# A new hand-written order of all steps in a windowed-attention and gated-MLP kernel on one core

## The chip, the core and the metric

The kernel runs on one core of a Trainium2 chip, in one launch. The core has five engines that run side by side, each through its own instruction queue in order: PE (TensorE, matmuls), DVE (VectorE), ACT (ScalarE), POOL (GpSimd) and SP (SyncE, which only issues DMAs here). DMAs are issued from SP's queue or from POOL's; 16 DMA engines carry them out. The metric is the device time of a whole run in microseconds (us), lower is better. Runs of this kernel on one chip differ by some tenths of a per cent.

## What is computed

Attention over 4 batches, 8 heads, 768 positions and 64 columns a head, with a window of 128 positions and 4 sink positions that every row sees; then a block with a spatial gate on its output x (4 x 768 x 512). Inputs and output are float32; the kernel computes in bfloat16 with float32 sums.

```python
scores = scale * np.matmul(q, k.transpose(0, 1, 3, 2))
is_sink = pos[None, :] < int(n_sink)
in_window = (rel >= 0) & (rel < int(window))
scores = np.where(is_sink | in_window, scores, -1000000000.0)
a = np.exp(scores - np.max(scores, axis=-1, keepdims=True))
a = a / (np.sum(a, axis=-1, keepdims=True) + 1e-09)
x = np.matmul(a, v)                      # heads side by side: B, S, 512
...
h = gelu_tanh(x @ w_in)                  # 512 -> 1024
u, v = h[..., :512], h[..., 512:]
v_n = (v - mean) / np.sqrt(var + 1e-06) * g_ln
v_s = np.einsum('ts,bsd->btd', w_sg, v_n) + b_sg[None, :, None]
out = x + (u * v_s) @ w_out
```

## The kernel before

The whole program is a list of 669 steps, `STEPS`, written out by hand. Each step is a name with indices (batch first) and at times the letter of an engine (A for ACT, D for DVE, P for POOL); a loop at L676 calls the function of that name for each in turn. An engine executes its own steps in the order of the list; semaphores hold it where a step needs another engine's result or a buffer that is still in use. So the list fixes two things: the order within each engine's queue, and which of the interchangeable engines does a copy, a mask or a product. It fixes no times.

The steps of one batch b, in the order of the data:

- Loads. For batch 0, q and k come in four pairs of heads through SP (LPQ, LPK, L245; 384 KB each, float32) and are cast to bfloat16 (CPQ, CPK, L199 to L204). For the other batches POOL issues tile loads LQ, LK (L225). v comes in two halves of four heads each (LVH, L271, POOL's queue); LC (L289, SP) loads the four sink rows of v, LG (L292) the gains. Weights: LW.0 and LW.1 the two halves of w_in (L277), LWS two halves of w_sg (L282), LWO w_out (L285), LB the bias b_sg (L301), all on POOL's queue.
- Turning q and k: TQ, TK on PE (L376 for batch 0, L382 for others), then a copy EQ, EK to SBUF; for batch 3 the DMA does it, DQ and DK on SP (L440).
- Scores: QK (L483; with a last index 1 a bias matmul at L478 puts the mask in, otherwise MK masks later), EX the exponentials on ACT (L488), MK the mask on DVE (L495) or on POOL (L498, L501). Sinks: KS, VSM on DVE, SK (L462), SX (L467). Index p of QK, EX, MK is the pair of heads, g the group of positions.
- AV sums the window and the sinks (L524, L528, L531), NR divides by the sum on DVE (L540, L541) and writes x. Batch 0 does this in three parts of two tiles of 128 positions, the others in two parts of three.
- x is turned: XT and XE in batch 0 (L550), XD by DMA on SP (L557) in the others, one for each half.
- MV (L566) multiplies by w_in's half for v and GV applies the gelu on ACT (L570); BN, RS (POOL, L588), NM and Z normalise v (Z on ACT L597 or DVE L600). MU (L607) and GU (L612) do the same for u. MV and MU come in groups g of two tiles.
- WT and WE turn w_sg once (L619). SP multiplies by it (L627; index hf is the half of the positions, dc the quarter of the columns), GT applies gain and bias on DVE (L632), GM multiplies by u on DVE or POOL (L637).
- OU (L644) multiplies by w_out, RA adds x on DVE (L648), ST stores (L667), SH stores in halves (L664). The very last tile goes in halves: OH (L657), RH (L661).
- Fillers: HM.n puts n warm matmuls (L190) ahead of the next step that takes a PSUM buffer. TBL (L309) lets ACT load the table of exp (E) or gelu (G) early; the compiler adds a load by itself wherever the next function needs another table. WARM, FILL, IDEN, MASK, MASK0, VSK, VSO and ZERO write constants at the start.

PSUM is used as two rings: two large buffers `sc` for QK, MV and MU in turn (freed by ACT's EX, GV, GU), and four small ones `mm` for all other matmul steps (freed mostly by DVE). A step takes the next buffer of its ring whatever the key, so the list also sets who waits for whose buffer. Output tiles pass through a ring of six buffers, `ot`, each free again when its store has landed. The batches overlap: while batch b is in its gate, batch b+1 is in its scores.

Of the kernel before, what the change touches and what calls it, by code (L numbers as in the profile page):

```python
# [17 lines left out]


STEPS = """  # L20
WARM LPQ.0 FILL LPK.0 LPK.1 LPQ.1 LPQ.2 LG MASK LPK.2 LPK.3 CPQ.0.A VSK LPQ.3 IDEN CPK.0.A IDEN2 MASK0 HM.9 TQ.0.0
# [694 lines left out]
```

## Time and profile before

| | us |
|---|---|
| median of 3 runs | 155.82 (155.35 to 155.89) |
| the profiled execution, whole | 155.89 |
| its span, first to last instruction | 154.2 |
| PE busy in it | 145.7 |
| DVE, ACT, POOL busy | 122.9, 100.0, 99.7 |

A profile comes from one execution; what lies between its whole time and its span is start and end of the launch. The granted clock of PE was 1.00 throughout. In the profile a row names source line, engine, operation and tiles; `PEld` is PE's weight load, which runs beside its matmuls. The page cuts the span into 40 slices and gives each engine's busy share in tenths. The chain of waits is followed back from the last instruction: at each step to what released it. Times inside an execution are counted from the span's start.

PE's first matmul starts at 1.25 us, the first AV at 16.56, the first MV at 23.45, the first SP at 38.91, the first OU at 54.20, the first step of batch 3's gate (SP.3.1.0) at 137.35; PE's last matmul ends at 150.5, and the last store is issued by 151.8.

### The profile page before, as it was taken

How to read it: one execution, taken by the hardware profiler on the slowest of the kernel's cores; microseconds unless marked ns; L12 is line 12 of the kernel's file. 1: busy time of each engine (PE TensorE's matmuls, PEld its weight loads, DVE VectorE, ACT ScalarE, POOL GpSimd, SP SyncE). 2: the span in 40 equal slices, each digit the busy share in tenths (PEclk: the TensorE clock that was granted, in tenths of full speed). 3: DMA queues.
4: the chain of work that ended last, by engine and by line, in shares of the span. 5: the costliest groups of instructions: out<-in, count | busy, mean ns of one | idle time of the engine just before them, and what ended most of it. 6: DMA issues, size and time to landing. Idle time of an engine off the chain costs nothing.

```text
span 154.2 us, 3867 instructions
## 1 busy us (share of the span) xinstructions
PE 145.7 (95%) x1540; PEld 94.5 (61%) x1554; DVE 122.9 (80%) x296; ACT 100.0 (65%) x117; POOL 99.7 (65%) x127
## 2 busy tenths in 40 slices
PE   6899899999999988999899999999999999999990
PEld 2355586879675765758466764486567644775550
DVE  4666889739989977797799887899789957867992
ACT  3699998799899766456987865369957122491000
POOL 4099799298999699999469769640798610400400
PEclk9999999999999999999999999999999999999999
DMA  4999999999999999999999399996510582410055
GB/s 158 305 351 157 154 195 204 166 189 211 148 141 154 185 155 140 147 150 156 156 223 250 81 276 177 185 190 81 211 72 1 105 221 73 150 54 20 0 203 206
DMA packets 87178, 24.67 MB, mean 160 GB/s; under 512 B 78772, under 2 KB 84920, under 8 KB 87160
## 3 DMA queue, kind: packets, MB, share of 16 engines
q0 software_dynamic: 64608, 11.01, 95.7%
q1 hardware_dynamic: 22552, 13.41, 33.0%
q8 instruction: 12, 0.20, 0.5%
q14 instruction: 6, 0.05, 0.1%
HBM read 24.81 MB, written 6.29 MB: 202 GB/s over the span
## 4 chain that ended last, share of the span: by engine, by line
PE 54%; POOL 18%; DMA 15%; ACT 4%; DVE 4%; issue 2%; SPq 1%; DVEq 0%; ACTq 0%; POOLq 0%
PE mm L627 15%; DMA v_sb<-in_v_dram 11%; PE mm L644 10%; PE sc L566 9%; PE sc L607 8%; POOL q L225 5%; POOL k L225 4%; DMA uT<-in_k_dram 4%; PE sc L483 4%; PE mm L524 3%; POOL v_sb L271 3%; PE mm L528 2%; POOL wsg_gated L637 2%; POOL P L498 2%; POOL P L501 2%
## 5 line engine op out<-in xcount | busy, mean ns | idle before, releaser
L488 ACT ACTIVATE P<-sc 128x1024 bf16<-128x1024 f32 (+1 forms) x48 | 43.4, 952 | 10.3 <-PE sc L483 10.1
L627 PE MATMUL mm<-wsgT,z 128*128 128x384 bf16 x192 | 34.4, 327 | 0.3 <-ACT z L597 0.3
L627 PEld LDWEIGHTS <-z 128*128 128x128 bf16 x192 | 17.6, 98 | 12.5 <-issue 0.7
L570 ACT ACTIVATE vt<-sc 128x1024 f32<-128x1024 f32 x12 | 12.3, 1027 | 18.4 <-PE sc L566 18.4
L632 DVE SCALAR_TENSOR_TENSOR gtmp<-mm,g_sb,b_bc 128x384 bf16<-128x384 f32 x32 | 19.0, 610 | 4.2 <-PE mm L627 4.0
L637 POOL TENSOR_TENSOR wsg_gated<-gtmp,uT 128x384 bf16<-128x384 bf16 x15 | 14.9, 1006 | 11.3 <-DVE gtmp L632 11.2
L607 PE MATMUL sc<-xT,w_in_sb 128*128 128x256 bf16 x192 | 22.1, 273 | 0.0
L566 PE MATMUL sc<-w_in_sb,xT 128*128 128x512 bf16 x92 | 21.8, 379 | 0.2
L644 PE MATMUL mm<-w_out_sb,wsg_gated 128*128 128x512 bf16 x85 | 21.2, 379 | 0.5
L498 POOL TENSOR_SCALAR_AFFINE_SELECT P<-P 128x512 bf16<-128x512 bf16 x21 | 13.7, 653 | 11.4 <-ACT P L488 11.4
L607 PEld LDWEIGHTS <-w_in_sb 128*128 128x128 bf16 x192 | 18.7, 98 | 2.9
L579 DVE BATCH_NORM_STATS2 st<-vt 128x6 f32<-128x512 f32 x24 | 15.4, 685 | 6.1 <-ACT vt L570 6.0
L541 DVE TENSOR_TENSOR x_sb<-mm,rcp 128x384 bf16<-128x384 f32 (+1 forms) x36 | 18.5, 513 | 1.2
L588 POOL TENSOR_TENSOR rs<-rs,neg_half 128x4 f32<-128x4 f32 (+1 forms) x8 | 7.1, 882 | 15.8 <-DVE rs L583 14.4
L225 POOL DMA_DIRECT2D k<-in_k_dram x18 | 16.4, 924 | 1.3 <-DMA v_sb<-in_v_dram 1.3
L648 DVE TENSOR_TENSOR ot<-mm,x_sb 128x512 f32<-128x512 f32 x23 | 15.4, 683 | 2.2 <-PE mm L644 2.2
L225 POOL DMA_DIRECT2D q<-in_q_dram x18 | 16.8, 956 | 0.0
L524 PE MATMUL mm<-v_sb,P 128*128 128x65 bf16 x192 | 16.1, 194 | 0.6 <-DVE x_sb L541 0.4
L524 PEld LDWEIGHTS <-P 128*128 128x128 bf16 x192 | 14.5, 97 | 2.5 <-DMA v_sb<-in_v_dram 0.6
L528 PE MATMUL mm<-v_sb,P 128*128 128x65 bf16 x160 | 15.4, 193 | 0.4 <-POOL P L501 0.4
L612 ACT ACTIVATE uT<-sc 128x1024 bf16<-128x1024 f32 x12 | 12.2, 1024 | 5.1 <-PE sc L607 5.1
L566 PEld LDWEIGHTS <-xT 128*128 128x128 bf16 x96 | 9.2, 98 | 10.1
(92 smaller groups left out, 242.9 us busy)
## 6 DMA issues: line engine op xcount, KB each, us to landing
out_dram<-ot SPq DMA_DIRECT2D x17, 256.0 KB, 2.5
v_sb<-in_v_dram POOLq DMA_DIRECT2D x8, 384.0 KB, 8.0
q<-in_q_dram POOLq DMA_DIRECT2D x18, 128.0 KB, 6.5
k<-in_k_dram POOLq DMA_DIRECT2D x18, 128.0 KB, 7.3
out_dram<-ot SPq DMA_DIRECT2D x14, 128.0 KB, 1.8
wsg_gated<-in_moe_w_sg_dram POOLq DMA_DIRECT2D x2, 576.0 KB, 8.4
w_in_sb<-in_moe_w_in_dram POOLq DMA_DIRECT2D x2, 512.0 KB, 9.0
uT<-in_q_dram SPq DMA_DIRECT2D x2, 384.0 KB, 3.0
```

The source lines that it names most:

```text
L225: return nc.gpsimd.dma_start(out=dst.rearrange("p (h d) -> p h d", h=H), in_=heads(src, b, i))
L488: nc.scalar.activation(out=P.new((b, p, g))[:, :, 0:w], in_=sc_ring[b, p, g][:, :, 0:w], func=AF.Exp, scale=scale)
L498: nc.gpsimd.affine_select(out=p4[:, :, :, 0:128], in_=p4[:, :, :, 0:128], compare_op=ALU.is_ge, fill=0.0, base=0, pattern=[[0, 2], [0, 2], ...
L524: nc.tensor.matmul(av[:, il, hl, :], pt[:, hl, c:c + 128], vb[:, h, i, :], start=first, stop=False)
L528: nc.tensor.matmul(av[:, il, hl, :], pt[:, hl, c:c + 128], vb[:, h, i - 1, :], start=False, stop=(i < 2 and il == n - 1 and hl == 1))
L541: nc.vector.tensor_mul(x_sb.get(b)[:, i0:i0 + n, 128 * p:128 * (p + 1)].rearrange("p t (h d) -> p t h d", h=2), av[:, :, :, 0:Dh], rcp[:, ...
L566: nc.tensor.matmul(hp[:, jl, :], xT[b][:, 2 * g + jl, c, :], w_in_sb[:, c, d_half:2 * d_half], start=(c == 0), stop=(c == KD - 1))
L607: nc.tensor.matmul(hp[:, dc // 2, 256 * (dc % 2):256 * (dc % 2 + 1)], w_in_sb[:, c, 128 * dc:128 * (dc + 1)], xT[b][:, 2 * g:2 * g + 2, c, :],
L627: nc.tensor.matmul(ps[:, 0:NH], z[b][:, si, 128 * dc:128 * (dc + 1)], wsgT[:, si, NH * hf:NH * (hf + 1)], start=(si == 0), stop=(si == NT ...
L632: nc.vector.scalar_tensor_tensor(out=gtmp.new((b, hf, dc)), in0=mm_ring["g", b, hf, dc][:, 0:NH], scalar=g_sb[:, dc:dc + 1], in1=b_bc[:, N ...
L637: (nc.vector if e == "D" else nc.gpsimd).tensor_mul(gated(b, hf)[:, dc, :], gtmp[b, hf, dc], uT[b][:, dc, NH * hf:NH * (hf + 1)])
L644: nc.tensor.matmul(ps, gated(b, hf)[:, dc, 128 * tl:128 * (tl + 1)], w_out_sb[:, dc, :], start=(dc == 0), stop=(dc == KU - 1))
```

## The change

All steps stand in a new order. The same work is done; no size, tile or buffer changes. With the order go these reassignments: batch 0's casts of q and k go from three on ACT, two on POOL and three on DVE to none, three and five; copies EK go from eight on ACT and two on DVE to three and seven, EQ from two and eight to five and five; GM from 17 on DVE and 15 on POOL to 20 and 12; WE, XE and Z change by one each; some MK change between DVE and POOL at equal numbers. Warm matmuls go from 21 to 19. TBL gets a second index, a number that only keeps the names apart, and stands at seven places, most of which no longer lie where the table changes; the compiler's own loads take their place. OH asks the ring whether the tile's buffer is taken, so that its halves can come in either order.

In the new list SP issues the pairs in the order q0, k0, LG, k1, q1, k2, q2, k3, q3 and LC behind them; LW.0 and LW.1 follow each other on POOL's queue with no load between.

The list's diff, cut; the lines left out are of the same kind:

```diff
--- before.py
+++ after.py
@@ STEPS @@
-WARM LPQ.0 FILL LPK.0 LPK.1 LPQ.1 LPQ.2 LG MASK LPK.2 LPK.3 CPQ.0.A VSK LPQ.3 IDEN CPK.0.A IDEN2 MASK0 HM.9 TQ.0.0
-TK.0.0 EQ.0.0.D EK.0.0.A VSO HM.4 QK.0.0.0 ZERO CPK.1.P QK.0.0.1.1 EX.0.0.0 LVH.0.0 EX.0.0.1 QK.0.0.2.1 CPQ.1.D TK.0.1
-EX.0.0.2 LC CPQ.2.D LVH.0.1 TQ.0.1 MK.0.0.0.D EK.0.1.A HM.1 TQ.0.2 EQ.0.1.D EQ.0.2.A HM.3 QK.0.1.0 CPK.2.A CPK.3.P
-QK.0.1.1.1 EX.0.1.0 LQ.1.0 CPQ.3.D TK.0.2 EX.0.1.1 TK.0.3 EK.0.2.D LQ.1.1 TQ.0.3 EK.0.3.A GTR EQ.0.3.D LW.0 HM.1
-QK.0.2.0 QK.0.2.1 EX.0.2.0 LK.1.0 KS.0 VSM.0 HM.3 SK.0.2 EX.0.2.1 SK.0.1 MK.0.2.0.D AV.0.0.0 LW.1 QK.0.3.0.1
-MK.0.1.0.D SX.0.1 SX.0.2 QK.0.3.1 MK.0.2.1.P GCP.D NR.0.0.0 EX.0.3.0 AV.0.0.1 AV.0.1.0 AV.0.1.1 NR.0.0.1 EX.0.3.1
-QK.0.1.2 NR.0.1.0 AV.0.2.0 AV.0.3.0 EX.0.1.2 MK.0.3.1.P NR.0.1.1 QK.0.2.2 AV.0.2.1 NR.0.2.0 EX.0.2.2 TQ.1.0 NR.0.3.0
-MK.0.1.2.P QK.0.3.2 AV.0.3.1 EQ.1.0.A NR.0.2.1 XT.0.0 NR.0.3.1 LWS.0 AV.0.0.2 EX.0.3.2 TBL.G AV.0.1.2 XE.0.0.D LK.1.1
-XT.0.1 MK.0.2.2.D MV.0.0 XE.0.1.A LK.1.2 NR.0.0.2 MK.0.3.2.D LK.1.3 NR.0.1.2 AV.0.2.2 AV.0.3.2 LQ.1.2 NR.0.2.2 GV.0.0
-MV.0.1 NR.0.3.2 LQ.1.3 BN.0.0 LWS.1 XT.0.2 GV.0.1 MU.0.1 XE.0.2.A BN.0.1 WT.0 GU.0.1 TK.1.0 MV.0.2 RS.0.1 EK.1.0.A
-LK.1.4 NM.0.1 WE.0.A WT.1 GV.0.2 LK.1.5 TK.1.1 MU.0.2 LB.P EK.1.1.A BN.0.2 Z.0.0.A LK.2.0 WT.2 GU.0.2 MU.0.0 WE.1.D
-RS.0.2 WE.2.D Z.0.1.A LQ.2.0 NM.0.2 Z.0.2.A Z.0.3.D Z.0.4.D WT.3 LQ.2.1 WT.4 GU.0.0 TBL.E WE.3.D WT.5 LQ.1.4 Z.0.5.D
-TQ.1.1 QK.1.0.0 EQ.1.1.D QK.1.1.0 LQ.1.5 SP.0.0.0 WE.4.D LK.2.1 EX.1.0.0 VSM.1 SP.0.0.1 WE.5.D EX.1.1.0 LVH.1.0
-GT.0.0.0 TK.1.2 KS.1 GT.0.0.1 QK.1.2.0 QK.1.3.0 EX.1.2.0 SP.0.0.2 LVH.1.1 GM.0.0.0.D EX.1.3.0 MK.1.2.0.D TQ.2.0
-EK.1.2.A LQ.2.2 QK.1.0.1 EQ.2.0.D QK.1.1.1 TQ.1.2 EX.1.0.1 GT.0.0.2 LWO SP.0.0.3 EQ.1.2.D EX.1.1.1 LK.2.2 MK.1.0.1.D
...
-EX.1.2.2 SP.0.1.3 NR.1.0.0 MK.1.1.2.P EX.1.3.2 NR.1.1.0 AV.1.2.0 AV.1.3.0 MK.1.0.2.P GT.0.1.3 QK.2.0.0 QK.2.1.0
-NR.1.2.0 EX.2.0.0 OU.0.0 MK.1.2.2.P NR.1.3.0 TK.2.1 RA.0.0 AV.1.0.1 XD.1.0 EK.2.1.A MK.1.3.2.P AV.1.1.1 NR.1.0.1
-AV.1.2.1 EX.2.1.0 GM.0.1.2.P NR.1.1.1 AV.1.3.1 NR.1.2.1 QK.2.2.0 LK.3.0 QK.2.3.0 EX.2.2.0 OU.0.1 NR.1.3.1 GM.0.1.3.P
-EX.2.3.0 TBL.G OU.0.2 XD.1.1 RA.0.1 GM.0.1.1.P TK.2.2 MK.2.3.0.D TQ.2.1 LVH.2.0 TQ.2.2 EQ.2.1.D MV.1.0 EQ.2.2.D LQ.3.0
-EK.2.2.D LQ.3.1 VSM.2 MU.1.0 GV.1.0 MK.2.1.0.D LVH.2.1 BN.1.0 MV.1.1 GU.1.0 LQ.3.2 RA.0.2 LQ.3.3 MK.2.0.0.D MV.1.2
-GV.1.1 MK.2.2.0.D LK.3.1 KS.2 LK.3.2 BN.1.1 MU.1.1 GV.1.2 LK.3.3 BN.1.2 RS.1.1 MU.1.2 GU.1.1 LQ.3.4 NM.1.1 Z.1.0.A
-RS.1.2 OU.0.3 GU.1.2 TBL.E LQ.3.5 NM.1.2 Z.1.1.D SK.2.0 Z.1.4.D QK.2.0.1 Z.1.2.D Z.1.3.A QK.2.1.1 Z.1.5.D OU.0.4
-RA.0.3 DK.3.0 SP.1.0.0 RA.0.4 SX.2.0 EX.2.0.1 SP.1.0.1 GT.1.0.0 DQ.3.0 EX.2.1.1 GM.1.0.0.D SP.1.1.0 MK.2.0.1.P
...
-EX.2.3.2 NR.2.3.0 QK.3.0.0 MK.2.3.2.P QK.3.1.0 GT.1.1.3 XD.2.0 EX.3.0.0 AV.2.0.1 MK.2.2.2.D AV.2.1.1 EX.3.1.0 NR.2.0.1
-AV.2.2.1 GM.1.1.3.P ST.0.1 NR.2.1.1 AV.2.3.1 ST.0.2 ST.0.5 GM.1.1.0.P SK.3.0 NR.2.2.1 QK.3.2.0 QK.3.3.0 NR.2.3.1
-EX.3.2.0 GM.1.1.2.P SP.1.0.2 EX.3.3.0 XD.2.1 SP.1.0.3 GT.1.0.2 SX.3.0 TBL.G MK.3.3.0.D MV.2.0 GM.1.0.2.P DK.3.1
-GM.1.1.1.D LK.3.4 MK.3.0.0.D OU.1.3 LVH.3.0 GV.2.0 OU.1.4 RA.1.3 LVH.3.1 OU.1.5 ST.1.3 RA.1.4 GT.1.0.3 MV.2.1 ST.1.4
-MK.3.1.0.D LK.3.5 BN.2.0 GM.1.0.3.P MV.2.2 GV.2.1 BN.2.1 MU.2.1 GV.2.2 BN.2.2 RS.2.1 MU.2.0 GU.2.1 NM.2.1 RA.1.5
-RS.2.2 MU.2.2 GU.2.0 NM.2.2 Z.2.4.D Z.2.5.D Z.2.0.A Z.2.1.D OU.1.0 GU.2.2 TBL.E Z.2.2.D MK.3.2.0.D OU.1.1 RA.1.0
...
-NR.3.2.0 NR.3.3.0 EX.3.3.2 TBL.G SP.2.0.3 MK.3.2.2.P GT.2.0.2 XD.3.0 AV.3.0.1 GT.2.0.3 MK.3.3.2.P AV.3.1.1 NR.3.0.1
-AV.3.2.1 GM.2.0.3.P NR.3.1.1 AV.3.3.1 SP.2.1.3 GM.2.0.2.D GM.2.1.1.P NR.3.2.1 OU.2.0 NR.3.3.1 GT.2.1.3 XD.3.1 OU.2.1
-RA.2.0 GM.2.1.3.P OU.2.2 GM.2.1.2.D SH.2.0.0 SH.2.0.1 RA.2.1 MV.3.0 RA.2.2 SH.2.1.0 SH.2.1.1 OU.2.3 GV.3.0 OU.2.4
-BN.3.0 MV.3.1 RA.2.3 RA.2.4 MV.3.2 SH.2.3.0 SH.2.3.1 GV.3.1 SH.2.2.0 SH.2.2.1 SH.2.4.0 SH.2.4.1 BN.3.1 OU.2.5 GV.3.2
...
-SH.2.5.0 SH.2.5.1 SP.3.1.0 GU.3.0 SP.3.1.1 GU.3.1 GT.3.1.0 SP.3.1.2 GM.3.1.0.D GT.3.1.1 SP.3.1.3 GM.3.1.1.D GT.3.1.2
-SP.3.0.0 GM.3.1.2.D SP.3.0.1 GT.3.0.0 GT.3.1.3 SP.3.0.2 GT.3.0.1 GM.3.1.3.P SP.3.0.3 GM.3.0.0.D GM.3.0.1.P GT.3.0.2
-OU.3.3 GM.3.0.2.D GT.3.0.3 OU.3.4 GM.3.0.3.D RA.3.3 OU.3.0 RA.3.4 ST.3.3 OU.3.1 RA.3.0 ST.3.4 OU.3.2 ST.3.0 RA.3.1
-OH.3.5.0 OH.3.5.1 ST.3.1 RA.3.2 ST.3.2 RH.3.5.0 SH.3.5.0 RH.3.5.1 SH.3.5.1
+WARM FILL IDEN LPQ.0 MASK MASK0 IDEN2 LPK.0 VSK CPQ.0.P CPK.0.D LG HM.9 TQ.0.0 EQ.0.0.D ZERO TK.0.0 LPK.1 VSO LPQ.1
+LVH.0.0 EK.0.0.A HM.3 QK.0.0.0 CPK.1.D CPQ.1.D LPK.2 EX.0.0.0 LPQ.2 HM.1 QK.0.0.1.1 LPK.3 EX.0.0.1 CPK.2.D TK.0.1
+LVH.0.1 QK.0.0.2.1 EK.0.1.A LK.1.1 CPK.3.P TQ.0.1 LQ.1.1 LPQ.3 LC CPQ.3.P EQ.0.1.A TK.0.2 CPQ.2.D TQ.0.2 QK.0.1.0
+EX.0.0.2 EK.0.2.D EX.0.1.0 TK.0.3 LQ.1.0 EQ.0.2.D EK.0.3.D QK.0.1.1.1 TQ.0.3 MK.0.0.0.D EX.0.1.1 LW.0 GTR KS.0
+EQ.0.3.A GCP.D QK.0.2.0 MK.0.1.0.D LW.1 QK.0.2.1 VSM.0 HM.1 AV.0.1.0 EX.0.2.0 HM.1 AV.0.0.0 SK.0.1 SK.0.2 EX.0.2.1
+HM.1 QK.0.3.0.1 SX.0.1 SX.0.2 NR.0.1.0 QK.0.3.1 MK.0.2.0.D AV.0.1.1 NR.0.0.0 AV.0.2.0 NR.0.1.1 AV.0.0.1 EX.0.3.0
+EX.0.3.1 HM.1 AV.0.3.0 MK.0.2.1.P QK.0.3.2 EX.0.3.2 NR.0.0.1 NR.0.2.0 QK.0.1.2 AV.0.0.2 AV.0.2.1 EX.0.1.2 NR.0.3.0
+XT.0.0 MK.0.3.1.P AV.0.3.1 MK.0.3.2.P NR.0.0.2 LB.P LK.1.0 NR.0.2.1 LQ.1.2 QK.0.2.2 XE.0.0.A NR.0.3.1 MK.0.1.2.D
+TQ.1.0 AV.0.3.2 XT.0.1 AV.0.1.2 NR.0.3.2 LWS.0 LQ.1.3 EX.0.2.2 EQ.1.0.A MV.0.0 LQ.2.0 MK.0.2.2.D LWS.1 XE.0.1.D
+NR.0.1.2 LK.1.2 AV.0.2.2 NR.0.2.2 GV.0.0 LK.1.3 MV.0.1 XT.0.2 MU.0.1 BN.0.0 GV.0.1 LQ.1.4 GU.0.1 XE.0.2.D BN.0.1
+MV.0.2 LQ.2.1 TK.1.0 GV.0.2 EK.1.0.D RS.0.1 MU.0.2 NM.0.1 BN.0.2 WT.1 WT.0 TBL.G.1 MU.0.0 Z.0.3.A LK.2.4 Z.0.1.A
+RS.0.2 NM.0.2 LK.2.0 WE.1.D Z.0.4.D LK.2.1 WE.0.A LQ.1.5 Z.0.2.D WT.2 WE.2.D Z.0.5.D Z.0.0.A HM.1 TQ.1.1 GU.0.2
+QK.1.0.0 WT.4 HM.1 SP.0.0.1 GU.0.0 EQ.1.1.D LK.1.4 TK.1.1 WT.3 WE.4.A LK.1.5 VSM.1 EK.1.1.D EX.1.0.0 GT.0.0.1 SP.0.0.0
+MK.1.0.0.D QK.1.1.0 QK.1.3.0 WE.3.D GT.0.0.0 GM.0.0.1.D WT.5 EX.1.1.0 TQ.2.0 QK.1.2.0 SP.0.0.2 EX.1.3.0 EX.1.2.0
+EQ.2.0.A QK.1.0.1 QK.1.3.1 MK.1.3.0.D KS.1 EX.1.0.1 WE.5.D GT.0.0.2 SP.0.0.3 LVH.1.0 GT.0.0.3 EX.1.3.1 LVH.1.1
...
+MK.1.2.1.P QK.1.2.2 AV.1.2.0 QK.1.3.2 NR.1.1.0 EX.1.2.2 SP.0.1.3 LK.2.3 MK.1.0.2.P MK.1.1.2.P NR.1.3.0 MK.1.2.2.D
+OU.0.0 NR.1.2.0 QK.2.0.0 EX.1.3.2 GT.0.1.3 QK.2.1.0 AV.1.2.1 RA.0.0 AV.1.0.1 NR.1.2.1 MK.1.3.2.P EX.2.1.0 EX.2.0.0
+NR.1.0.1 LK.2.2 XD.1.0 OU.0.1 AV.1.1.1 KS.2 LQ.2.2 QK.2.3.0 EX.2.3.0 QK.2.2.0 AV.1.3.1 GM.0.1.3.P TQ.2.2 EX.2.2.0
+RA.0.1 NR.1.1.1 GM.0.1.0.P OU.0.2 LVH.2.1 ST.0.0 MV.1.0 NR.1.3.1 VSM.3 LQ.2.3 GV.1.0 LVH.2.0 GM.0.1.1.D TK.2.1 MU.1.0
+MK.2.2.0.D VSM.2 XD.1.1 GU.1.0 LK.3.3 EQ.2.2.D MV.1.1 EK.2.1.D GM.0.1.2.D LK.3.0 MV.1.2 LQ.3.4 GV.1.1 RA.0.2 LQ.3.0
+MU.1.1 GV.1.2 MK.2.3.0.D BN.1.0 TQ.2.1 BN.1.1 BN.1.2 LK.3.5 MU.1.2 RS.1.1 NM.1.1 EQ.2.1.D RS.1.2 OU.0.3 NM.1.2 LQ.3.2
+MK.2.1.0.D LQ.3.5 GU.1.1 TK.2.2 Z.1.2.A Z.1.4.D Z.1.1.A LK.3.1 RA.0.3 OU.0.4 SK.2.0 LK.3.2 GU.1.2 QK.2.0.1 EK.2.2.D
+Z.1.0.A Z.1.3.D LQ.3.3 Z.1.5.D QK.2.1.1 MK.2.0.0.D EX.2.0.1 DK.3.0 SP.1.0.0 RA.0.4 EX.2.1.1 GT.1.0.0 SP.1.0.1 SP.1.1.0
...
+NR.2.1.0 MK.2.2.1.P QK.2.3.2 RA.0.5 EX.2.1.2 KS.3 EX.2.3.2 ST.0.3 AV.2.3.0 MK.2.0.2.P GT.1.1.2 MK.2.2.2.D NR.2.3.0
+MK.2.1.2.P AV.2.2.0 SP.1.1.3 DQ.3.2 AV.2.0.1 NR.2.2.0 QK.3.1.0 EX.3.1.0 QK.3.3.0 MK.2.3.2.P GM.1.1.1.P AV.2.1.1
+GT.1.1.3 AV.2.2.1 NR.2.0.1 EX.3.3.0 SP.1.0.3 AV.2.3.1 NR.2.1.1 QK.3.0.0 QK.3.2.0 NR.2.2.1 NR.2.3.1 GM.1.1.0.P GT.1.0.3
+EX.3.0.0 DQ.3.1 SK.3.0 SX.3.0 XD.2.0 GM.1.1.2.D GM.1.1.3.D SP.1.0.2 TBL.E.1 XD.2.1 EX.3.2.0 OU.1.3 MV.2.0 MK.3.1.0.D
+GV.2.0 MV.2.1 GV.2.1 GT.1.0.2 MV.2.2 DK.3.1 GM.1.0.2.P BN.2.0 BN.2.1 ST.0.2 MU.2.1 GV.2.2 LK.3.4 MK.3.3.0.D BN.2.2
+GU.2.1 MU.2.2 ST.0.5 ST.0.1 MU.2.0 RS.2.1 NM.2.1 RA.1.3 RS.2.2 Z.2.3.D GM.1.0.3.D LVH.3.0 NM.2.2 Z.2.1.A OU.1.5
+Z.2.0.D Z.2.5.D OU.1.1 GU.2.2 OU.1.0 GU.2.0 Z.2.4.A RA.1.5 QK.3.0.1 QK.3.2.1 MK.3.2.0.D Z.2.2.D MK.3.0.0.D RA.1.1
+OU.1.4 EX.3.0.1 SP.2.0.0 EX.3.2.1 LVH.3.1 RA.1.4 DK.3.2 MK.3.0.1.P ST.0.4 RA.1.0 GT.2.0.0 QK.3.0.2 GM.2.0.0.D QK.3.1.1
...
+NR.3.2.0 EX.3.3.2 GT.2.1.2 SP.2.0.1 GM.2.1.1.P AV.3.3.0 SP.2.0.2 NR.3.1.0 GM.2.1.0.P GT.2.0.1 SP.2.0.3 AV.3.0.1
+NR.3.3.0 AV.3.1.1 GT.2.0.2 GM.2.1.2.D EX.3.2.2 MK.3.3.2.P GT.2.0.3 NR.3.0.1 TBL.G.2 AV.3.3.1 MK.3.2.2.P NR.3.1.1
+ST.1.3 GM.2.0.3.D GM.2.0.2.P XD.3.0 TBL.E.2 AV.3.2.1 ST.1.5 SP.2.1.3 GM.2.0.1.D NR.3.3.1 OU.2.1 NR.3.2.1 TBL.G.3
+OU.2.2 GT.2.1.3 MV.3.0 GM.2.1.3.D GV.3.0 OU.2.4 RA.2.2 OU.2.3 RA.2.1 ST.1.4 OU.2.5 XD.3.1 RA.2.4 RA.2.5 BN.3.0 MV.3.1
+GV.3.1 MV.3.2 BN.3.1 GV.3.2 SH.2.2.0 RS.3.1 BN.3.2 MU.3.2 MU.3.0 SH.2.1.1 SH.2.2.1 GU.3.2 NM.3.1 Z.3.0.D Z.3.2.D
...
+RA.2.0 SH.2.5.1 TBL.E.3 SP.3.1.1 GT.3.1.2 GT.3.1.1 SH.2.0.0 SH.2.3.1 SH.2.0.1 GT.3.1.0 SH.2.4.1 SP.3.1.3 GM.3.1.1.D
+GM.3.1.2.P GT.3.1.3 GM.3.1.3.D GM.3.1.0.P SP.3.0.1 SP.3.0.3 GT.3.0.1 SP.3.0.0 SP.3.0.2 GT.3.0.3 SH.2.5.0 GM.3.0.1.D
+OU.3.3 GT.3.0.0 OU.3.4 GT.3.0.2 GM.3.0.0.D SH.2.3.0 GM.3.0.2.D GM.3.0.3.P RA.3.3 SH.2.1.0 OU.3.0 RA.3.4 RA.3.0 OU.3.1
+ST.3.3 OU.3.2 ST.3.4 ST.3.0 RA.3.1 OH.3.5.1 RA.3.2 OH.3.5.0 ST.3.1 RH.3.5.0 ST.3.2 SH.3.5.0 RH.3.5.1 SH.3.5.1 TBL.G.4
...
-    def TBL(func):
+    def TBL(func, turn):
         nc.scalar.activation(out=touch, in_=neg_half[:, 0:1], func=AF.Exp if func == "E" else AF.Gelu_apprx_tanh)
...
     def OH(b, t, h):
         hf, tl = t // 3, t % 3
-        ps = mm_ring["o", b, t] if h else fresh(mm_ring, ("o", b, t))
+        ps = mm_ring["o", b, t] if ("o", b, t) in mm_ring.held else fresh(mm_ring, ("o", b, t))
```

## The prediction

> **What bounds the kernel now.** First the page: busy shares, slices, the chain by engine.
>
> ```profile
> span 154.2 us, 3867 instructions
> PE 145.7 (95%) x1540; PEld 94.5 (61%) x1554; DVE 122.9 (80%) x296; ACT 100.0 (65%) x117; POOL 99.7 (65%) x127
> PE   6899899999999988999899999999999999999990
> PE 54%; POOL 18%; DMA 15%; ACT 4%; DVE 4%; issue 2%; SPq 1%; DVEq 0%; ACTq 0%; POOLq 0%
> ```
>
> PE is busy nearly throughout; only the first eighth, the slices around 55 us and the last two show holes. Next the chain of waits in order of time (start, us, what), its beginning and its end:
>
> ```profile
> 1.81 5.80 DMA uT<-in_k_dram
> 7.69 0.79 POOL k L204
> 8.48 8.04 DMA v_sb<-in_v_dram
> 16.56 0.25 PE mm L524 x3
> ...
> 126.23 1.73 PE mm L644 x8
> 127.96 3.45 PE sc L566 x16
> 131.41 0.86 PE mm L644 x4
> 132.28 5.24 PE sc L607 x48
> 137.52 7.80 PE mm L627 x48
> ```
>
> Until 16.6 us the chain is data: k's second pair, its cast on POOL, then V's first half, for which AV waits. From 76 us it is PE alone. The x-counts price PE's steps: MV 1.73, MU 5.24/3 = 1.75, SP 7.80/8 = 0.975, OU 0.86. From the timeline, first matmul to the next step's first: a QK 0.18 to 0.32, an AV 0.18, 0.36 or 0.54 (6, 10 or 15 matmuls), a turn of one group 0.34 to 0.54, one warm matmul 0.22. What a step takes beyond the least of its kind I call a gap. All steps at their least are 131.9 us, warm and bias matmuls 6.4, gaps 11.0: 5 of these before 19.5 us, 3.2 in nine places of at least 0.2 after 30 us, the rest some 0.09 at each change of operand shape. So behind the start a new order can win 3.2 us at most. The waits list names three such places (total, times, longest):
>
> ```profile
> PEld L524 <- DMA v_sb<-in_v_dram: 0.6, 1, 0.6
> PEld L644 <- DMA w_out_sb<-in_moe_w_out_dram: 0.4, 1, 0.4
> PE mm L528 <- POOL P L501: 0.4, 1, 0.4
> ```
>
> Last, DMA by window (length, then busy PE, PEld, DVE, ACT, POOL; clock, DMA share, GB/s), and one window of idle ACT:
>
> ```profile
> 9.00:11.00 2.00, 1.79 (x41) 1.29 (x43) 1.51 (x3) 2.00 (x3) 2.00 (x2) 1.00 1.04 383
> 11.00:12.00 1.00, 1.00 (x13) 0.37 (x8) 0.99 (x2) 0.98 (x3) 0.90 (x2) 1.00 1.29 173
> 97.00:99.50 2.50, 2.50 (x13) 1.16 (x12) 1.95 (x6) 1.02 (x1) 1.74 (x2) 1.00 1.87 192
> 102.00:104.00 2.00, 2.00 (x21) 1.79 (x20) 1.78 (x8) 1.28 (x2) 0.89 (x2) 1.00 2.45 157
> 120.00:124.00 4.00, 3.95 (x42) 2.42 (x41) 3.90 (x11) 0.02 (x1) 2.78 (x4) 1.00 0.43 82
> ```
>
> Pair loads alone move 383 GB/s, POOL's strided loads alone 157: two regimes. POOL's loads land in order of issue, a q or k tile each 0.85 to 0.9 us, V's halves 3.3, w_in's 2.5, w_sg's 2.8, and from 11 to 60 us that row hardly ever runs empty.
>
> **The change, part by part.** PE's work is the same but for warm matmuls: 21 before, 19 after.
>
> *Pairs and casts.* SP gets q0 k0 g k1 q1 k2 q2 k3 q3; the 2 KB of g move ahead of k1 (0 to 0.46 us, its issue; 0.1 taken, the pairs being bound by bandwidth). The sink rows stand behind all pairs in both. Pairs land at 3.8, 5.0, 7.6, 8.7, 9.7, 10.8, 11.8 and 12.8 by the trace's semaphores. ACT loses its three casts (0.83 each); the first QK then follows k0's landing by the cast on DVE 0.56, a turn 0.5 and its copy 0.80: 7.0, not 7.35. k3 and q3 are cast on POOL with LQ.1.1's issue between: 11.8 + 0.8 + 0.9 + 0.83 = 14.3 for q3, against 13.4. The turn of q3 comes 0.4 late, but PE has nothing else to win there, since AV waits for V. Cost 0; 0.5 if V lands sooner.
>
> *V's loads.* They leave POOL behind only CPQ.0, but v_sb's ones (ZERO on DVE, behind EQ.0.0) hold them to 6.5 + 0.3 = 6.8, against 8.48. When do they land? In the packet records the three DMA engines that lag with the pairs run these every 62 to 64 ns from 11.6 to 12.2 with no V packet among them (V's rate is then that of 13 engines), so V starts on each engine when its pairs are through. By that V still lands at 16.5 and 19.4: taken 0, with 1.6 sooner (8.48 - 6.85) as the other bound. The Trainium skill (DMA: Bandwidth & Descriptors, "Queues, rings and completion order") has each DMA engine go round-robin between rows, a packet of 9 to 17 descriptors at a time; by it V would take most of the pairs' time, which would make the sum that of rival C. Here the lagging engines' records speak against it, while the stores at 97 us speak for it.
>
> *PE behind V.* Between V's second half (AV.0.2.0) and the first MV lie, in addition, AV.0.0.1 0.37, QK.0.1.2 0.32 and a warm matmul 0.22, which lay in the wait for V before: +0.9 (AV.0.3.2, 0.36, only changes sides of MV). Warm matmuls ahead of TQ.1.1 and SP.0.0.1: +0.44. The gap at TK.1.0 (0.21) goes: -0.2. w_in's halves in a row bring the second 0.9 sooner, but MU.0.1 found it 1.8 us early: 0.
>
> *POOL's queue before RS.0.1.* It now stands behind LB (0.56), eight tile issues of 0.87 and two of 0.76 from MK.0.3.2's end near 22.6: free at about 31.7. BN.0.1 ends near 31.2, so NM.0.1 and the Z are 0.5 late. ACT is at GV.0.2 till 33.4, so 0; without that cover 0.5, and SP.0.0.1 would wait for Z.
>
> *ACT tables.* The program holds 12 table loads for 8 (1.28 us, with its touch 1.48). Two of the four more stand where ACT was busy 0.02 of 4 us (the window above), two behind GU.3.1, where nothing follows. 0; 3.0 if MV.3.0 came that much sooner.
>
> *52 to 64 us.* OU.0.0 waits 0.30 there (w_out), TK.2.1 0.54, AV.1.3.1 0.73, OU.0.1 0.23: 1.8. The new order deals OU and QK out among the AV, and turns TK.2.1, TQ.2.1 and TK.2.2 only behind MV.1.0: -1.8. But these turns were what covered x's transposes. XD.1.0 took 5.6 us from issue (55.49) to its last packet, XD.1.1 4.7; with NR.1.2.0 at 55.4 and NR.1.3.1 at 60.0, MV.1.0 waits about 0.4 and MV.1.1 0.5: +0.9 (0 to 2.0).
>
> *Batch 1's SP.* SP.1.0.0 waited 0.54 for Z; the turns are now between: -0.5. Three waits of OU and AV for POOL (0.23, 0.22, 0.22) go with MK and GM dealt anew; OU.3.3 no longer waits for a GM of POOL: -0.65.
>
> *MV.2.1 follows MV.2.0 at once.* Before, three OU (2.6 us) stood between. XD.2.1 is issued behind NR.2.3.1, and the six transposes of x take 3.7 to 5.2 to land; MV.2.0 and OU.1.3 hide 2.6 of that and NR's lead 0.6: +0.5 (0.2 to 0.9). LVH.3.0 and 3.1 go out near 101 and 102.4 instead of 94 and 95.5; at 6.6 to 9.8 us, AV.3.2.0 at 111 may wait: +0.2 (0 to 0.6).
>
> Sum: 0.9 + 0.44 - 0.2 - 1.8 + 0.9 - 0.5 - 0.65 + 0.5 + 0.2 = -0.2 us. On the profiled execution (span 154.2, whole time 155.89) that is 155.7; its runs have the median 155.82, so 155.6.
>
> **The rivals.** A is the sum.
>
> *B, the covers are too thin: slower.* SP waits in order and the transposes run beside POOL's loads. Under such loads they ran at 214 to 232 packets in half a microsecond instead of 550. If XD.1.0, XD.1.1 and XD.2.1 each run as slowly, the three MV wait at their upper bounds, 2.0 + 0.9, and AV.3.2.0 0.6: 1.9 over A, 157.5. It decides as soon as one takes over 5 us. For it: the turns that covered them are gone. Against: before, no MV waited at all, and at 90 us POOL's row is empty.
>
> *C, V takes the pairs' place: slower.* In 97 to 99.5 us stores ran with V's loads at 26 packets in half a microsecond instead of 100. If the pairs fared like that from 8.5 us on, an engine would pass 3.25 pair packets per us while V's and one tile's 448 run at 47 per us (9.5 us): 31 of its 48 to 60, so q3 would land near 19.5, not 12.8; with both casts behind it on POOL the first MV would be 5.5 late: 161. Against: the three engines' records above, with the pairs queued first as here (SP has issued all by 6.5).
>
> *D, V lands sooner: faster.* V was on the chain till 16.6. If its 1.6 us earlier issue counts, the first AV comes at PE's own pace (15.6), the 0.9 behind V's second half is again in its shadow, and all later transposes start sooner: 1.6 under A, 154.0. For it: V's issue is on the chain. Against: V's first packet came 2.6 us after its issue, as the pairs ended.
>
> That the named part does little (sink rows already last, w_in not waited for) is in A.
>
> **How the numbers follow.** A 0.39, B 0.26, C 0.10, D 0.25. 0.5% of 155.82 is 0.78 us, about what a measurement of this kernel tells from no change: bounds 155.04 and 156.60. A's own range is 154.6 to 156.8: 0.07 faster, 0.27 same, 0.05 slower. D: 0.23 and 0.02 same. B: 0.03 same, 0.23 slower. C slower. Together 0.30, 0.32, 0.38. The range holds A whole, D but its end and B with its bounds: 153.8 to 158.6; C is left out.
>
> **What would show it.** Right: V's first half near 16.5 in spite of an issue near 6.9; the first MV at 24 to 25; no gap over 0.3 at 52 to 60 but waits of MV.1.0 or 1.1 for x's transposes; SP.1.0.0 0 to 1 us sooner than 75.65; a wait of MV.2.1. C shows as q3's landing behind 15, D as an AV before 16. It is wrong if a queue is held that I took as free: POOL's before RS.0.1, or SP's DK.3.2 ahead of ST.0.4, whose buffer RA.1.0 needs.

## The result, and the profile after

| | before, four executions | after, four executions |
|---|---|---|
| median, us | 155.58 (154.69 to 155.89) | 162.93 (162.22 to 165.54) |
| ratio to before, 95% interval | | 1.047 (1.040 to 1.053) |
| profiled execution, whole / span | 155.89 / 154.2 | 162.22 / 160.5 |

Slower by 7.3 us; the forecast was 155.6, its range ended at 158.6. The ratios here and below, each to before run beside it, leave out executions more than 1.5% above the fastest of their kernel (here the 165.54); the medians do not. The page of the changed kernel first: span, busy time, PE's slices and its granted clock.

```profile
span 160.5 us, 3855 instructions
PE 147.0 (92%) x1537; PEld 94.7 (59%) x1552; DVE 127.7 (80%) x302; ACT 102.1 (64%) x117; POOL 96.6 (60%) x125
...
PE   6888699999998999829999999999999999999990
...
PEclk9999999999999999995999999999999999999999
```

Two things are new. The slice at 68 us has a 2 where PE stood at 9, and in the next one the clock row, which had a 9 throughout before, has a 5. The chain of waits over this stretch (start, us, what) names the cause of the first:

```profile
61.97 0.57 DVE x_sb L541
...
62.56 8.74 DMA xT<-x_sb
...
71.35 3.62 PE sc L566 x11
...
75.19 2.35 PE sc L607 x16
```

XD.1.1, the DMA transpose of x's second half, goes out at 62.56, when DVE has finished NR.1.3.1 (L541) and lands 8.74 us later. In before it took 5.2, the longest that the view of L557 there gives from issue to landing:

```profile
DMA to landing us min/median/max: 3.7/4.4/5.2
```

MV.1.1 (L566) had started at 66.65 and stands still after four of its eight matmuls. The profile lacks a few matmul records: the row of 11 behind the wait holds twelve, the last four of MV.1.1 and the eight of MV.1.2. From 71.35 to MU.1.1's start at 75.19 they take 3.84 us, and MU.1.1 takes 2.19 to the next step, where eight matmuls of MV cost 1.73 and an MU 1.75. The windows of 2 us (length, busy PE, PEld, DVE, ACT, POOL; clock, DMA share, GB/s) show why, one of before first, then four of after:

```profile
68.00:70.00 2.00, 2.00 (x14) 1.15 (x12) 1.65 (x4) 1.30 (x2) 2.00 (x3) 1.00 2.43 155
...
68.00:70.00 2.00, 0.00 (x0) 0.00 (x0) 0.54 (x3) 0.00 (x0) 1.42 (x2) 1.00 2.00 156
70.00:72.00 2.00, 0.65 (x3) 0.31 (x4) 0.00 (x0) 0.00 (x0) 0.00 (x0) 1.00 2.46 156
72.00:74.00 2.00, 2.00 (x8) 0.82 (x7) 0.52 (x1) 1.02 (x1) 0.00 (x0) 0.67 2.70 153
74.00:76.00 2.00, 1.78 (x7) 0.97 (x7) 1.15 (x5) 0.57 (x1) 0.73 (x1) 0.50 2.42 154
```

PE is idle from 67.7 to 71.35, the granted clock falls to 0.5 behind that and is back by 76.1. DMA moves about 156 GB/s all the while, the rate that was read before as that of POOL's strided loads. So POOL's row (its DMA queue) was full while XD.1.1 moved. The packets by queue tell it directly (packets, MB, share of 16 engines; q0 carries POOL's loads, q1 SP's transfers). In before, while XD.1.1 moved, 62.4 to 64.6 us:

```profile
q1 hardware_dynamic: 1383, 0.35, 109.4%
q0 software_dynamic: 190, 0.02, 19.4%
```

In after from 65 to 69 us, and then from 69.2 to 71.3:

```profile
q0 software_dynamic: 1915, 0.24, 93.9%
q1 hardware_dynamic: 1479, 0.38, 72.7%
...
q0 software_dynamic: 2490, 0.32, 239.2%
q1 hardware_dynamic: 62, 0.01, 4.9%
```

About 1,400 packets of the transpose took 4 us in place of 2.2, with more of POOL's packets than their own beside them. The last 62, of which 32 are only 4 bytes long, came one by one up to 70.56, and the landing followed at 71.30.

The balance: from MV.1.0's start to SP.1.0.0's took 13.2 us before (62.45 to 75.65) and 20.0 after (62.72 to 82.72). The 6.8 between them are 3.84 of MV.1.1's wait (its fifth matmul was due at 67.51 and came at 71.35), 1.68 of half clock (MV.1.2 2.97 for 1.73, MU.1.1 2.19 for 1.75) and 1.33 for the three turns that moved into the stretch. Ahead of it the order is 0.3 later. Behind it the order is 0.65 shorter, of which 0.54 is SP.1.0.0's wait for Z, which is gone.

### The profile page after: what moved, and what is told of

Same layout as the page of the kernel before. It is cut to its first block, busy times and chain, and to the rows that moved or that the text cites. A ratio compares the mean times of both kernels' runs of the same rounds, so it can differ in the third digit from the quotient of the medians.

```text
span 160.5 us, 3855 instructions
## 1 busy us (share of the span) xinstructions
PE 147.0 (92%) x1537; PEld 94.7 (59%) x1552; DVE 127.7 (80%) x302; ACT 102.1 (64%) x117; POOL 96.6 (60%) x125
## 4 chain that ended last, share of the span: by engine, by line
PE 70%; DMA 14%; DVE 10%; issue 1%; POOL 1%; SPq 0%; DVEq 0%
PE mm L627 18%; PE sc L607 12%; PE sc L566 12%; PE mm L644 11%; DMA v_sb<-in_v_dram 7%; DMA xT<-x_sb 5%; PE sc L483 5%; PE mm L524 3%; DVE x_sb L541 3%; DVE P L495 3%; DMA uT<-in_k_dram 3%; PE mm L528 2%; PE mm L382 2%; PE mm L531 2%; PE mm L619 1%
## 5 line engine op out<-in xcount | busy, mean ns | idle before, releaser
L627 PE MATMUL mm<-wsgT,z 128*128 128x384 bf16 x192 | 34.9, 326 | 0.1
L566 PE MATMUL sc<-w_in_sb,xT 128*128 128x512 bf16 x93 | 23.0, 393 | 4.1 <-DMA xT<-x_sb 3.9
L570 ACT ACTIVATE vt<-sc 128x1024 f32<-128x1024 f32 x12 | 12.3, 1024 | 18.6 <-PE sc L566 16.6
L607 PE MATMUL sc<-xT,w_in_sb 128*128 128x256 bf16 x192 | 22.7, 276 | 0.2 <-issue 0.2
L541 DVE TENSOR_TENSOR x_sb<-mm,rcp 128x384 bf16<-128x384 f32 (+1 forms) x36 | 18.5, 513 | 1.2
L566 PEld LDWEIGHTS <-xT 128*128 128x128 bf16 x96 | 9.4, 100 | 15.5 <-DMA xT<-x_sb 4.9
L524 PE MATMUL mm<-v_sb,P 128*128 128x65 bf16 x192 | 16.6, 194 | 1.3 <-DMA v_sb<-in_v_dram 1.3
L637 POOL TENSOR_TENSOR wsg_gated<-gtmp,uT 128x384 bf16<-128x384 bf16 x12 | 10.9, 921 | 10.6 <-DVE gtmp L632 10.6
L612 ACT ACTIVATE uT<-sc 128x1024 bf16<-128x1024 f32 x12 | 12.1, 1018 | 5.9 <-PE sc L607 5.9
L528 PE MATMUL mm<-v_sb,P 128*128 128x65 bf16 x160 | 15.8, 193 | 0.0
```

What stands on the lines that cost most here:

```text
L524: nc.tensor.matmul(av[:, il, hl, :], pt[:, hl, c:c + 128], vb[:, h, i, :], start=first, stop=False)
L528: nc.tensor.matmul(av[:, il, hl, :], pt[:, hl, c:c + 128], vb[:, h, i - 1, :], start=False, stop=(i < 2 and il == n - 1 and hl == 1))
L541: nc.vector.tensor_mul(x_sb.get(b)[:, i0:i0 + n, 128 * p:128 * (p + 1)].rearrange("p t (h d) -> p t h d", h=2), av[:, :, :, 0:Dh], rcp[:, ...
L566: nc.tensor.matmul(hp[:, jl, :], xT[b][:, 2 * g + jl, c, :], w_in_sb[:, c, d_half:2 * d_half], start=(c == 0), stop=(c == KD - 1))
L607: nc.tensor.matmul(hp[:, dc // 2, 256 * (dc % 2):256 * (dc % 2 + 1)], w_in_sb[:, c, 128 * dc:128 * (dc + 1)], xT[b][:, 2 * g:2 * g + 2, c, :],
L627: nc.tensor.matmul(ps[:, 0:NH], z[b][:, si, 128 * dc:128 * (dc + 1)], wsgT[:, si, NH * hf:NH * (hf + 1)], start=(si == 0), stop=(si == NT ...
```

## Experiments

Theory: POOL's loads issued around XD.1.1's 62.56 (LVH.2.1 at 61.3, LVH.2.0 at 63.6, tiles to 68.5) stretch it, PE idles, the idle time halves the clock. Rivals: DVE's late NR.1.3.1; the store ahead of XD.1.1; the turns taken away as cover; the rest of the order. The diffs show steps of the list, cut, against after; before_loads is against before, late_repeat against loads_late, z_early against before_front.

**loads_clear.** V's loads early, two products from DVE to POOL.

```diff
 LK.2.5
+LVH.2.1 LVH.2.0
 ...
-LVH.2.1 ... LVH.2.0 GM.0.1.1.D ... GM.0.1.2.D
+GM.0.1.1.P GM.0.1.2.P
 LK.3.3
```

> The changed kernel with V's two loads for batch 2 (LVH.2.1, LVH.2.0) moved on POOL's queue to behind LK.2.5, where its row has room, and two products GM.0.1.1 and GM.0.1.2 moved from DVE to POOL ahead of LK.3.3, so that the tile loads behind them go out about 3 us later against XD.1.1. Theory (XD.1.1 took 8.74 us because these loads share the 16 DMA engines): XD.1.1 lands 4.5 to 5.5 us after its issue, MV.1.1 waits at most 1 us, no stretch of half clock follows, and the whole time falls by 4.5 to 5.5 us, to 157.5 to 158.5. Rival (the issue of XD.1.1 is late because DVE comes late to NR.1.3.1; loads matter little): issue at 62.5 as before, wait of at least 3 us, 161.5 or more.

Measured: 165.81 us, ratio 1.065 (1.060 to 1.070). The row had no room there: V's loads, issued at 49.2 and 51.2, landed only at 62.7 and 68.4, beside both transposes, and delayed everything queued behind them. In the profiled execution, the slowest of the four (168.98; the others 165.2 to 166.2), XD.1.0 took 9.5 us, XD.1.1 11.0, and the chain shows a third victim, the tile of k that TK.2.1 turns:

```profile
59.94 14.27 DMA k<-in_k_dram
...
74.25 1.03 PE mm L382 x8
```

The expectation failed, since the loads were moved from one transpose onto the other. It bears out that loads stretch transposes, but says nothing on DVE.

**before_loads.** The same collision made in the kernel before, with its own DVE order.

```diff
 MK.1.3.2.P
+LVH.2.0 LVH.2.1
 ... XD.1.1 ...
-LVH.2.0 ... LVH.2.1
```

> The kernel before with only LVH.2.0 and LVH.2.1 moved on POOL's queue to behind MK.1.3.2, so that they are issued at about 58.4 and 59.9, just ahead of XD.1.1 (59.93). Theory: XD.1.1 takes 7 to 8.7 us in place of 4.7, MV.1.1 (first matmul at 65.93) waits 1 to 2.7 us, with a slow clock behind it if PE idles long enough: 157 to 160. Rival (late DVE): XD.1.1 is issued where it was, MV.1.1 waits under 0.3, 155.4 to 156.2.

Measured: 161.6 us, ratio 1.036 (1.028 to 1.044), more than expected. PE's timeline (start, us, what, idle before it and its releaser) shows the same picture as in after, here with XD.1.1 issued at 58.64, earlier than in before:

```profile
64.64 1.03 PE L566 MATMUL sc<-w_in_sb,xT 128*128 128x512 bf16 x3
70.97 5.30 PE L566 MATMUL sc<-w_in_sb,xT 128*128 128x512 bf16 x12 [5.31 <-DMA xT<-x_sb]
```

XD.1.1 took 12.3 us. So a late DVE is not needed for the loss: two loads of V issued just ahead of the transpose (57.1 and 58.5) are enough, and the covers that before has don't prevent it.

**warm_wait.** Fillers in the wait.

```diff
+HM.15
 MV.1.1
```

> The changed kernel with 15 warm matmuls (0.22 us each, 3.3 us) ahead of MV.1.1, so that PE does not idle in its wait. Theory (the half clock of 3.4 us follows from the idle time): XD.1.1 still lands near 71.3 and MV.1.1 ends as late, but the granted clock stays 1.0, MV.1.2 takes 1.73 and MU.1.1 1.75: 1.9 us less, about 161.0. Rival (the clock drops whatever PE does there): half clock at 72 to 76 again, 162.5 to 163.2.

Measured: 162.53 us, ratio 1.043 (1.035 to 1.050). In the profiled execution the clock stayed at 1.00; the twelve matmuls of MV behind the landing took 2.60 us in place of 3.84, MU.1.1 1.75 in place of 2.19. So it is PE's idle time that halves the clock. The time did not follow, and came out in the rival's range: XD.1.1 took 9.3 us in this execution, 0.7 more by its landing, SP.1.0.0 came 1.0 sooner than in after (81.72), and MV.2.1 then waited for XD.2.1, which took 5.4 us in place of 3.7; the span is again 160.5. 161.0 was wrong: a microsecond won at 80 us was lost at 100.

**store_behind.**

```diff
-ST.0.0
 ... XD.1.1
+ST.0.0
```

> The changed kernel with ST.0.0 moved on SP's queue from between XD.1.0 and XD.1.1 to behind XD.1.1. Theory (POOL's loads are the main load on the engines, the store's 256 KB a small part): XD.1.1 takes 7.5 to 8.7 us, the whole time falls by 0 to 1 us, 162 to 163. Rival (the store is what slows the transposes): XD.1.1 takes at most 6 us, MV.1.1 waits under 1.5, 158 to 160.

Measured: 163.09 us, ratio 1.049 (1.043 to 1.054); XD.1.1 8.7, as in after. The store is not the cause.

**loads_late.** The loads held back by work that DVE had. On POOL the masks of group 0 leave out the exception of the sink rows.

```diff
 LQ.2.3
+GM.0.1.1.P GM.0.1.2.P MK.2.2.0.P MK.2.3.0.P
+LVH.2.1 LVH.2.0 LK.3.0 LK.3.1 RS.1.1 LQ.3.0 RS.1.2 LQ.3.4 LQ.3.5 LQ.3.2 LQ.3.3 LK.3.2
 MK.2.0.1.P MK.2.1.1.P
+LK.3.3
 ...
+LK.3.5
 LK.3.4
```

> The changed kernel with POOL's queue dealt anew around XD.1.1: behind LQ.2.3 first two products and two masks that DVE had (GM.0.1.1, GM.0.1.2, MK.2.2.0, MK.2.3.0; 0.9 and 1.2 us each, together some 4 us), then LVH.2.1, LVH.2.0, LK.3.0, LK.3.1 ahead of RS.1.1, the other tile loads behind RS.1.1 and RS.1.2. V's loads are so issued near 66 in place of 61.3, and their packets can't meet those of XD.1.1 (issued near 62.5, its packets at 65 to 67). Theory (loads on the row at the same time make the wait, which makes the half clock): XD.1.1 lands at most 5.2 us after its issue, MV.1.1 waits at most 1.2 us, no half clock, whole time 156 to 158.6. Rival (the rest of the stretch from 62 to 82 us, DVE above all, costs as much by itself): 161 or more with no long wait for xT.

Measured: 157.24 us, ratio 1.011 (1.003 to 1.020): 5.7 us less than after. XD.1.1 was issued still later, at 64.44, landed in 4.4 us, and the chain has PE alone:

```profile
64.11 1.73 PE sc L566 x8
...
66.28 1.75 PE sc L607 x16
68.03 3.37 PE sc L566 x15
...
71.45 1.91 PE sc L607 x16
```

MV.1.1 and MV.1.2 are the one row of 3.37. The theory's range held. It is still 1.6 above before: in the profiled execution MV.1.0 starts at 63.94, 1.5 later than in before, the stretch to SP.1.0.0 is 1.4 longer, about what the three turns in it take, and 0.8 is won behind. Why this front part comes late was not tried. Two things were changed at once, so three more runs take them apart.

**dve_relief.** The same four steps taken from DVE, with the loads in their old place.

```diff
 LK.3.5
+GM.0.1.1.P GM.0.1.2.P MK.2.2.0.P MK.2.3.0.P
 RS.1.1
```

> The changed kernel with the same two products and two masks moved from DVE to POOL as in loads_late, but behind LK.3.5, so that all loads keep their place. The two masks on POOL leave out the exception of the sink rows in group 0. Theory: DVE's relief alone is worth little, XD.1.1 still takes 8 to 9.3 us, 161.5 to 164. Rival (DVE's load is the cause): 159 or less.

Measured: 163.35 us, ratio 1.041 (1.031 to 1.050); XD.1.1 9.7. The four executions took 161.14, 162.78, 163.91 and 163.92, and the interval overlaps that of after: DVE's relief alone is not shown to be worth anything. The four steps stand behind NR.1.3.1 on DVE, so XD.1.1's issue stays at 62.6; that rival is answered by before_loads (an earlier issue, the same loss) and loads_late (a later one, no wait).

**late_repeat.** The loads as in loads_late, DVE with its masks; two products stay off DVE.

```diff
-MK.2.2.0.P MK.2.3.0.P
+GM.0.1.1.P GM.0.1.2.P GM.0.1.3.P
 LVH.2.1
```

> POOL's queue as in loads_late, but both masks stay on DVE; in their place POOL does three of batch 0's products (GM.0.1.1, GM.0.1.2, GM.0.1.3) a second time, 2.6 us, which changes no value and holds V's loads back to about 66. Theory (the time of the loads decides, not DVE's relief, and the loads must still go out before RS.1.1): XD.1.1 lands at most 5.5 us after its issue, no half clock, 157 to 159. Rival (DVE's relief is needed as well, as the 162 of v_behind could be read): 160.5 or more.

Measured: 159.08 us, ratio 1.021 (1.017 to 1.025), just over its range. XD.1.1 landed in 3.8 us and MV.1.1 did not wait for it. So the place of the loads, with the two products off DVE, is worth 3.9 us, and the two masks off DVE, once the loads are out of the way, perhaps another 1.8 (the intervals of the two runs overlap). PE's timeline shows where PE waits for DVE and ACT here, ahead of QK and SP.1.0.0 (lines stand one further in this kernel):

```profile
78.57 0.40 PE L484 MATMUL sc<-qT,kT 64*128 64x256 bf16 x6 [0.57 <-ACT uT L613]
...
80.61 2.29 PE L628 MATMUL mm<-wsgT,z 128*128 128x384 bf16 x13 [0.35 <-DVE z L601]
```

**v_behind.** The loads pushed further.

```diff
 LQ.2.3
+GM.0.1.1.P GM.0.1.2.P LK.3.0 LK.3.1
 RS.1.1
+LVH.2.0
 RS.1.2
+LVH.2.1 LQ.3.0 LQ.3.4 LQ.3.5
 MK.2.0.1.P MK.2.1.1.P
+LQ.3.2 LQ.3.3 LK.3.2 LK.3.3
 ...
+LK.3.5
 LK.3.4
```

> The changed kernel with all its masks left on their engines: POOL's queue has behind LQ.2.3 only GM.0.1.1, GM.0.1.2 (taken from DVE) and LK.3.0, LK.3.1, and both of V's loads stand behind RS.1.1, which itself can only run after MV.1.1. Theory (V's loads on the row beside XD.1.1 make the loss): XD.1.1 lands at most 5.5 us after its issue, MV.1.1 waits at most 1.2 us, no half clock, 156.5 to 158.8. Rival (the masks moved off DVE were what helped in the run before): a wait of 2.5 us or more, 160.5 or more.

Measured: 161.98 us, ratio 1.041 (1.033 to 1.048). XD.1.1 took 5.4, MV.1.1 waited 1.2, no half clock: what was expected of the stretch came. The whole time did not; it lies in the rival's range, but without the rival's wait. The waits list from 74 to 100 us has new ones (total, times, longest):

```profile
PEld L627 <- DVE z L600: 1.5, 2, 0.8
PEld L462 <- DMA qT<-q: 1.2, 1, 1.2
```

RS.1.2 stood behind a load's issue of 1.5 us, and batch 3's q came late for its own transposes. A load that leaves one place has to go to another.

**covers_back.** The turns as cover again.

```diff
 MU.1.0
+TQ.2.1 TK.2.2
 MV.1.1
```

> The changed kernel with the turns TQ.2.1 and TK.2.2 (and their copies) put back ahead of MV.1.1, as cover. Theory (XD.1.1's landing is set by the loads): XD.1.1 still takes 8 to 9.3 us and MV.1.1's last operand comes near 71.3, the turns take 0.9 of the wait of 3.6, with or without a half clock of one window: 161 to 162.3. Rival (taking the turns away is what cost the time): wait of MV.1.1 under 1, no half clock, 158 or less.

Measured: 164.56 us, ratio 1.055 (1.045 to 1.065), slower than both expectations. The chain shows that the cover itself had to wait:

```profile
62.00 1.40 POOL v_sb L271
63.40 9.32 DMA q<-in_q_dram
...
72.76 1.46 PE mm L382 x12
```

TQ.2.1 needs LQ.2.3. In before this tile was issued at 46.9, here behind LVH.2.1 at 63.4, so it lands as late as XD.1.1 (72.7 and 72.4).

**before_front and after_front.** One list up to SP.1.0.0, the other behind it.

```diff
+steps of one list up to SP.1.0.0, in its order
+all steps that are left, in the order of the other list
```

> Order of before for all its steps up to SP.1.0.0, then the remaining steps in the order of the changed kernel. Theory (all of the loss lies between 62 and 82 us; from SP.1.0.0 to PE's end the changed kernel took 74.2 us, before 74.85): 0.7 us less than before, 154.3 to 155.5. Rival (the later part of the new order costs too): 156.5 or more.

> Order of the changed kernel for all its steps up to SP.1.0.0, then the remaining steps in the order of before. Theory: it holds the whole loss, XD.1.1 takes 8 to 9.3 us, MV.1.1 waits 3 to 4.5 us, a half clock of one or two windows follows, 162 to 165. Rival (the later part costs): 160 or less.

Measured: before_front 155.81 us, ratio 1.002 (0.998 to 1.006); after_front 163.03, ratio 1.047 (1.040 to 1.055). The whole loss lies ahead of SP.1.0.0. The 0.7 that the later part should win was not seen, and before_front came out between its two expectations: in the profiled execution SP.1.0.0 stood 0.93 us for batch 1's Z.

**z_early.** That gap closed.

```diff
 NM.1.1
+Z.1.1.D Z.1.2.D
 ...
 GU.1.2
+Z.1.3.A
 TBL.E
```

> The order of before_front with three of batch 1's Z moved: Z.1.1 and Z.1.2 on DVE behind NM.1.1 (where DVE stood idle for 1.4 us) and Z.1.3 on ACT ahead of the load of exp's table. In before_front the gap at SP.1.0.0 was 0.93 us with DVE's Z as what ended it. Expected: that gap falls to 0.2 or less, all else as in before_front (155.8): 154.8 to 155.3. If another wait takes its place: 155.6 or more.

Measured: 154.71 us, ratio 0.9945 (0.9906 to 0.9984), a little under its range; the gap at SP.1.0.0 is gone. This is the fastest of all: the order of before up to SP.1.0.0 with three steps moved, the new order behind it.

All runs in one view (issue, landing counted from it, and half clock ahead of PE's last matmul, all of the profiled execution; median of all executions):

| kernel | XD.1.1 issued | landing, us | half clock, us | median |
|---|---|---|---|---|
| before | 59.93 | 5.2 | 0 | 155.6 |
| z_early, before_front | 60.3, 59.5 | 5.2, 5.1 | 0 | 154.7, 155.8 |
| late_repeat | 64.2 | 3.8 | 0 | 159.1 |
| loads_late | 64.4 | 4.4 | 0 | 157.2 |
| v_behind | 64.4 | 5.4 | 0 | 162.0 |
| store_behind | 62.7 | 8.7 | 6.8 | 163.1 |
| after | 62.6 | 8.7 | 3.4 | 162.9 |
| after_front | 61.9 | 9.1 | 6.8 | 163.0 |
| covers_back | 63.2 | 9.2 | 6.8 | 164.6 |
| warm_wait | 62.7 | 9.3 | 0 | 162.5 |
| dve_relief | 62.6 | 9.7 | 6.8 | 163.4 |
| loads_clear | 63.0 | 11.0 | 13.7 | 165.8 |
| before_loads | 58.6 | 12.3 | 6.8 | 161.6 |

## Why the prediction was wrong, point by point

The step that failed is "52 to 64 us", in its term for x's transposes, "+0.9 (0 to 2.0)". It named the right danger, that the turns were what covered the transposes, and mis-sized it. MV.1.0's part, 0.4, came out at 0.44, in part by luck: XD.1.0 was issued at 57.5, where NR.1.2.0 had been put at 55.4, and PE was late as well. MV.1.1's part, summed as 0.5, measured 3.84 of wait and 1.68 of half clock. Three inputs were off.

- *Landing.* It put in XD.1.1's 4.7 from before. That row was taken while 190 packets of POOL passed beside it. In before V's two loads go out behind XD.1.1 (59.93), at 62.3 and 65.5; in the new order one goes out 1.3 us ahead of it and one 1.1 us behind, ahead of its first packets. The text counted queue slots ahead of RS.0.1 and did not do the same here. Loads around the transpose gave 8.7 to 12.3 us, loads held back 3.8 to 5.4.
- *Issue.* It took NR.1.3.1 as done at 60.0; it ended at 62.5, for DVE has hardly any idle time from 53 to 67 us in the new order (13.53 of 14 us busy). That moved the issue into V's loads. An issue at 62.56 with 5.2 us to land would have released MV.1.1 at 67.8, 0.3 after its fifth matmul was due; an issue at 60.0 with 8.74 us, 1.2 after. Only both together make 3.84.
- *The clock.* No term stood for what an idle PE costs afterwards.

A second term of the same step failed too, the "-1.8" for the gaps. All four are gone, but the time was not won. From the first MV to MV.1.0 before took 39.00 us and after 37.84, 1.16 less. At their least times PE's steps there take 1.25 less (three turns and AV.0.3.2 moved out, two warm matmuls in); with the sum's gaps and waits it should have been 2.85 less. PE stood idle for 1.11 us in both. Of the new gaps, 0.44 is MV.1.0's wait and 0.64 that of QK.1.0.2, behind SK.1.0, for DVE's copy of k; the rest is not traced. Up to SP.1.0.0's start the terms add to +0.24 us and 7.07 was measured. Of the 6.8 between them 5.0 lie in MV.1.1 and the clock, 1.7 between the first MV and MV.1.0.

The other steps:

- *Pairs and V's loads.* V's first half landed at 15.6 (issue 7.31 and 8.3 us), not 16.5; the second at 19.45 (19.4 predicted). The first AV started at 15.63. V's first packet came at 10.85, 3.5 us after its issue, and the last packet of the pairs at 11.82 (11.12 and 12.20 in before), so the reading that V starts as the pairs end holds. Why the half landed 0.9 sooner is not shown.
- *PE behind V.* First MV at 24.88, in the 24 to 25 that was named; against before +1.43, of which 0.36 is AV.0.3.2, which only changes sides. The rest is 1.07, where 0.9 was summed.
- *RS.0.1, ACT tables: 0.* No cost was seen. SP.0.0.1 came at 39.15, the first SP before at 38.91, and SP.3.1 to PE's end took 13.2 in both.
- *SP.1.0.0.* Its own wait is gone (-0.5), though it comes 7 us later.
- *MV.2.1, AV.3.2.0.* No wait in after, below the 0.2 and at the 0 of their ranges; warm_wait shows MV.2.1's at 1.15 when XD.2.1 takes 5.4.
- *Rival B* had the mechanism (transposes beside POOL's loads) and the sign. Its slow rate, 214 to 232 packets in half a microsecond, is close to the 204 of after. Its 157.5 was too small all the same: it gave both MV of batch 1 a wait of 2.0 at most, where MV.1.1 alone had 3.84, and it had no slow clock. *C* is refuted: q3 landed at 12.5, not behind 15. *D*'s sign came, an AV before 16, but not by D's mechanism, as V's packets still began with the pairs' end; and the second half still sets the first MV.

## What to carry to other kernels

When a new order moves a load ahead of a transfer that the critical engine waits for, price that transfer under the load, not by its row in the old order: here 5.2 became 8.7 to 12.3 us. Price a late issue and a slow landing together, since the one made the other worse. Look on every queue at what stands just ahead of each transfer with little slack, and at when the covers' own inputs are issued. Here a wait of 3.8 us on PE cost another 1.7 by the slow clock behind it.
